# A Fourier mix and a gated feed-forward on one core: first columns in halves, one weight copy moved, last products in another order

## The chip, the cores and the metric

The kernel runs on one core of a Trainium2 chip. The metric is the device time in microseconds (us). The profile's span, from the first to the last instruction, is about 1.85 us shorter (616.8 us of time had a span of 614.9). Engines: PE is TensorE, PEld its weight loads, DVE is VectorE, ACT is ScalarE, POOL is GpSimd, and SP is SyncE, which issues most of the transfers. "Clock" is the granted clock of TensorE, 1.00 for full and 0.50 for half.

## The reference

```python
X = np.fft.fft(x, axis=1)            # x: 8 x 3008 x 256
X = np.fft.fft(X, axis=2)
h = X.real.reshape(24064, 256)
g, val = h @ w_gate, h @ w_val       # 256 x 1536 each
out = (gelu(g) * val) @ w_out        # 1536 x 256, float32
```

## The kernel before

The transform is done with matmuls: a fold of the input on VectorE (GpSimd for later batches), a first stage (`s1`), a second (`ch`, which gives the tile Z), and a turn (`tp_e`) that gives even columns E and odd columns O of 128 x tokens. The feed-forward needs, for each of 12 slices of the hidden width, a gate product (E, O, and O with "minus" weights for the mirrored tokens) and a value product. GELU runs on ScalarE, the products with it on VectorE and GpSimd, and layer 2 goes to `out`. The opening builds the first columns and a part of the weights; later work is put into numbered slots between the matmuls of the feed-forward.

The parts that matter here (cuts marked):

```python
def psum(tag):
    bufs = {"g": 2, "v": 3, "o": 1, "dft": 2}[tag]          # 8 banks
...
def osb_tile():
    return work([128, 2, C], FP32, "osb", 3, "out_sb")      # three output buffers
...
# opening(): warm matmuls keep TensorE busy before there is work
warm(16)
...
columns = t_columns()                                       # ten small matmuls
...
s1(0, 2, 0)(); s1(0, 2, 1)()
...
warm(6)
...
warm(1)
s1(0, 0, 0)(); s1(0, 0, 1, "V")()
make_w(0, 0, 256, m_at=minus, tag="o", copy_at=copies)()    # gate weights, matmuls only
t_write()
for pp in range(2):
    ch(0, pp, qs=(0,))(); ch(0, pp, "V", qs=(1,))()
copies.pop()()                                              # gate copy, ScalarE
make_w(1, 0, 256, m_at=minus, m_engine="V", tag="v", copy_at=copies)()
tp_e(0, 0, 0, "A", tag="v")()                               # E out by ScalarE
tp_e(0, 0, 1, "V", tag="dft")()                             # O out by VectorE
copies.pop()(); minus[0](); minus[1]()
...
# layer 2 of the very last chunk: sub = 128 tokens, sign 0 direct, sign 1 mirrored
subs = [nsub - 1, *range(nsub - 1)] if last(ci) else range(nsub)
...
if last(ci):
    osb = osb_tile()
    if sign == 0:   # VectorE copies, both stores issued by SyncE
    else:           # ScalarE copies, first store by ScalarE, second by SyncE
```

## Time and profile before

The time is 616.64 us (median of 3 runs, 616.6 to 617.27). I cut the span at events: each is the start of an instruction, except the Z copy, which counts from its end. (The yw matmuls are twelve one-column matmuls that stand in slot 6.)

| stretch, us | before |
|---|---|
| start to the first fold on VectorE (its loads have landed) | 8.26 |
| first fold to the end of the last Z copy by VectorE | 8.09 |
| last Z copy to the first value matmul | 1.82 |
| first value matmul to the yw matmuls (slot 6) | 12.72 |
| yw matmuls to the last layer-1 matmul | 568.56 |
| last layer-1 matmul to the last matmul | 11.19 |
| last matmul to the end | 4.29 |
| span | 614.93 |

In the lines of a timeline the columns are start, duration, engine, line, operation, output<-input, and in brackets the idle time before and what ended it. Here are two more lines of the kernel before that the argument needs later: the start of the first fold, and (last line) ScalarE's last output copy.

```profile
8.26 0.19 DVE L221 TENSOR_TENSOR eo_sb<-x_stage,xb 94x8 bf16<-94x8 f32 x1
...
610.95 0.38 ACT L794 ACTIVATE out_sb<-ps_g 128x256 f32<-128x256 f32 x1 [2.24 <-DMA out_dram<-out_sb]
```

### The profile page before, as it was taken

What the parts mean: (1) busy time and instruction counts of PE and PEld (TensorE: products, weight loads), DVE (VectorE), ACT (ScalarE), POOL (GpSimd) and SP (SyncE); (2) the same over time, 40 slices, a digit from 0 to 9 for tenths busy, and PEclk for the clock granted to TensorE, in tenths of its full rate; (3) what the DMA queues carried; (4) which work ended last, traced back from release to release, by engine and by line L of the source; (5) the groups of instructions that cost most, each with busy time, mean ns of one, the idle gap of its engine ahead of it and who ended that gap; (6) DMA issues with size and microseconds to landing.
All of it is one profiled execution on the core that took longest, in us unless ns stands there. A gap on an engine that the chain in (4) does not pass through costs nothing.

```text
span 614.9 us, 12747 instructions
## 1 busy us (share of the span) xinstructions
PE 605.4 (98%) x4181; PEld 406.9 (66%) x4229; DVE 577.3 (94%) x941; ACT 425.0 (69%) x824; POOL 508.9 (83%) x513
## 2 busy tenths in 40 slices
PE   8999999999999999999999999999999999999997
PEld 4466666666666666666666666666666666666666
DVE  8799999999999999999999999999999999999992
ACT  6888677777776777667766677666776676666661
POOL 8999899999987999789997899869997655565551
PEclk8999999999999999999999999999999999999999
DMA  9962834547253364532553344533213223111123
GB/s 175 200 137 57 237 95 117 141 116 189 80 144 92 100 163 119 140 100 58 157 150 94 106 107 107 146 102 100 64 49 77 62 87 78 42 46 47 37 51 83
DMA packets 52466, 65.40 MB, mean 106 GB/s; under 512 B 7629, under 2 KB 47278, under 8 KB 50004
## 3 DMA queue, kind: packets, MB, share of 16 engines
q1 hardware_dynamic: 45472, 49.03, 30.5%
q0 software_dynamic: 6608, 15.29, 11.7%
q8 instruction: 33, 0.54, 0.4%
q10 hardware_dynamic: 320, 0.26, 0.2%
q14 instruction: 33, 0.27, 0.2%
HBM read 39.65 MB, written 30.17 MB: 114 GB/s over the span
## 4 chain that ended last, share of the span: by engine, by line
PE 94%; DVE 2%; issue 1%; DMA 1%; ACT 1%; SPq 1%; POOL 0%; DVEq 0%; POOLq 0%; ACTq 0%
PE ps_o L778 39%; PE ps_g L681 29%; PE ps_v L681 20%; PE ps_dft L562 2%; PE ps_dft L598 2%; DMA out_dram<-out_sb 1%; PE ps_dft L451 1%; SPq L675 1%; PE ps_o L847 0%; PE ps_dft L542 0%; ACT gelu_sb L705 0%; ACT gelu_sb L714 0%; DVE v_sb L751 0%; POOL h_sb L753 0%; PE ps_dft L603 0%
## 5 line engine op out<-in xcount | busy, mean ns | idle before, releaser
L753 POOL TENSOR_TENSOR h_sb<-gelu_sb,v_sb 128x512 bf16<-128x512 bf16 (+1 forms) x280 | 319.9, 1147 | 87.0 <-DVE v_sb L751 79.0
L778 PE MATMUL ps_o<-Wo_sb,h_sb 128*128 128x256 bf16 (+1 forms) x2232 | 334.3, 272 | 0.0
L778 PEld LDWEIGHTS <-h_sb 128*128 128x128 bf16 (+1 forms) x2304 | 228.6, 100 | 111.2 <-POOL h_sb L753 1.0
L733 DVE SCALAR_TENSOR_TENSOR ve_sb<-EB_sb,yw,ps_v 128x512 f32<-128x512 bf16 (+1 forms) x280 | 206.3, 737 | 18.6 <-PE ps_v L681 16.6
L705 ACT ACTIVATE gelu_sb<-ps_g 128x512 bf16<-128x512 f32 (+1 forms) x288 | 169.3, 588 | 78.1 <-PE ps_g L681 62.9
L749 DVE TENSOR_TENSOR h_sb<-gelu_sb,ps_v 128x512 bf16<-128x512 bf16 (+1 forms) x280 | 190.0, 678 | 0.7
L681 PEld LDWEIGHTS <-W_sb 128*128 128x128 bf16 x1440 | 138.4, 98 | 78.0 <-issue 1.7
L751 DVE SCALAR_TENSOR_TENSOR v_sb<-ve_sb,ps_v 128x512 f32<-128x512 f32 (+1 forms) x280 | 187.4, 669 | 0.0
L714 ACT ACTIVATE gelu_sb<-ps_g 128x512 bf16<-128x512 f32 (+1 forms) x288 | 168.6, 585 | 0.0
L681 PE MATMUL ps_g<-O_sb,W_sb 128*128 128x512 bf16 (+1 forms) x530 | 159.1, 374 | 2.7 <-DVE O_sb L610 0.3
L681 PE MATMUL ps_g<-E_sb,W_sb 128*128 128x512 bf16 (+1 forms) x287 | 107.6, 375 | 0.7 <-ACT gelu_sb L714 0.5
L681 PE MATMUL ps_v<-O_sb,W_sb 128*128 128x512 bf16 (+1 forms) x288 | 108.0, 375 | 0.0
L681 PE MATMUL ps_v<-E_sb,W_sb 128*128 128x512 bf16 (+1 forms) x288 | 107.9, 375 | 0.0
L798 ACT ACTIVATE out_sb<-ps_o 128x512 f32<-128x512 f32 x92 | 55.0, 598 | 34.2 <-PE ps_o L778 34.1
L229 POOL TENSOR_TENSOR eo_sb<-ab_sb 94x512 bf16<-94x512 f32 (+1 forms) x70 | 77.7, 1112 | 0.4
L565 ACT ACTIVATE S_sb<-ps_dft 96x512 bf16<-96x512 f32 x56 | 33.2, 592 | 29.7 <-PE ps_dft L562 29.7
L222 POOL TENSOR_TENSOR ab_sb<-x_raw,x_raw 94x508 f32<-94x508 f32 (+1 forms) x30 | 33.0, 1101 | 0.0
L225 POOL TENSOR_TENSOR ab_sb<-x_raw,x_raw 94x508 f32<-94x508 f32 (+1 forms) x30 | 33.0, 1100 | 0.0
L562 PE MATMUL ps_dft<-eo_sb,G 94*96 94x256 bf16 x119 | 22.3, 272 | 0.0
L608 ACT ACTIVATE E_sb<-ps_dft 128x512 bf16<-128x512 f32 (+1 forms) x23 | 13.6, 590 | 12.0 <-PE ps_dft L598 12.0
L608 ACT ACTIVATE O_sb<-ps_dft 128x512 bf16<-128x512 f32 (+1 forms) x22 | 13.0, 590 | 11.6 <-PE ps_dft L598 11.1
L163 POOL DMA_INDIRECT x_raw<-in_x_dram,idx x18 | 17.2, 957 | 2.9 <-issue 0.8
(151 smaller groups left out, 207.6 us busy)
## 6 DMA issues: line engine op xcount, KB each, us to landing
out_dram<-out_sb SPq DMA_DIRECT2D x364, 64.0 KB
x_raw<-in_x_dram SPq DMA_DIRECT2D x10, 768.0 KB
Z_sb<-z SPq DMA_DIRECT2D x7, 768.0 KB
z<-S_sb SPq DMA_DIRECT2D x7, 576.0 KB
EB_sb<-yrow SPq DMA_DIRECT2D x6, 376.2 KB
z<-S_sb SPq DMA_DIRECT2D x7, 192.0 KB
x_raw<-in_x_dram SPq DMA_DIRECT2D x2, 640.0 KB
x_stage<-in_x_dram SPq DMA_DIRECT2D x1, 768.0 KB
```

Source lines behind the costliest of these rows:

```text
L229: eng.tensor_tensor(_sub(eo, [[C, nj], [1, 128]], j0 * C + g * 128), ab(0, 0, [[1, 128]]), ab(1, 0, [[1, 128]]), op=op)
L562: nc.tensor.matmul(ps[:96, q * C : (q + 1) * C], G[:, j, :], _sub(eo, [[1, C]], j * C), start=(j == js[0]), stop=(j == js[-1]))
L565: nc.scalar.activation(_sub(st["S"], [[1, 512]], (4 * jg + 2 * half) * C, part_num=96), ps[:96, :], AF.Copy)
L681: nc.tensor.matmul(ps[:, :n], W[nm, part][:, fs], src, start=start, stop=stop, **kw)
L705: nc.scalar.activation(gl[:, 0, :n], pg[:, :n], AF.Gelu)
L714: nc.scalar.activation(_sub(gl, [[-1, n]], TOK + n - 1), pg[:, :n], AF.Gelu)
L733: nc.vector.scalar_tensor_tensor(ve[:, :n], EB_bufs[b][:, c0 : c0 + n], yw[:, fc : fc + 1], pv[:, :n], op0=ALU.mult, op1=ALU.add)
L749: nc.vector.tensor_tensor(st["h"][:, fc, 0, :n], gl[:, 0, :n], pv[:, :n], op=ALU.mult)
L751: nc.vector.scalar_tensor_tensor(_sub(vv, [[-1, n]], n - 1), ve[:, :n], 2.0, pv[:, :n], op0=ALU.mult, op1=ALU.subtract)
L753: nc.gpsimd.tensor_tensor(st["h"][:, fc, 1, :n], gl[:, 1, :n], vv[:, :n], op=ALU.mult)
L778: nc.tensor.matmul(pso[:m, half], st["h"][:, fc, sign, h0 : h0 + m], Wo_sb[:, fc, :], start=(fc == 0 and not (first and sign)), stop=(fc = ...
L798: nc.scalar.activation(_sub(osb, [[1, 2 * C]], 0, part_num=m), pso[:m, :], AF.Copy)
```

## The change

Its intent: bring the first gate and value matmuls forward by taking E and O out of two banks each with both engines; use ScalarE's idle time for the gate copy; drop a warm matmul; relieve ScalarE of one minus copy; and in the last layer 2 put a group between the first one and the one that waits for GpSimd.

```diff
-    def tp_e(b, gi, g=0, engine="A", tag=None):
+    def tp_e(b, gi, g=0, engine="A", tag=None, part=slice(0, 4)):
 ...
-            for pair, o, n in pairs(gi):
+            for pair, o, n in pairs(gi)[part]:
                 nc.tensor.matmul(...)
             if b == 0 and g == 1:
-                for pair, o, n in pairs(gi):
+                for pair, o, n in pairs(gi)[part]:
                     nc.tensor.matmul(ps[0:1, o : o + n], ...)
-            n = chunk_len[gi]
-            dst = _sub(EO_bufs[b][g], [[1, n]], chunk_off[gi])
+            o, n = pairs(gi)[part][0][1], sum(w for _, _, w in pairs(gi)[part])
+            dst = _sub(EO_bufs[b][g], [[1, n]], chunk_off[gi] + o)
 ... (the copies read ps[:, o : o + n] for ps[:, :n])
-            subs = [nsub - 1, *range(nsub - 1)] if last(ci) else range(nsub)
-            l2s = [... for s in subs for g in range(2) for f in range(0, NFC, L2P)]
+            order = [(s, g) for s in range(nsub) for g in range(2)]
+            if last(ci):
+                order = [(nsub - 1, 0), (0, 0), (nsub - 1, 1), *order[1:-2]]
+            l2s = [... for s, g in order for f in range(0, NFC, L2P)]
 ...
-        warm(1)
         s1(0, 0, 0)()
 ...
         make_w(0, 0, 256, m_at=minus, tag="o", copy_at=copies)()
+        copies[0]()
         t_write()
 ...
-        copies.pop()()
         make_w(1, 0, 256, m_at=minus, m_engine="V", tag="v", copy_at=copies)()
-        tp_e(0, 0, 0, "A", tag="v")()
-        tp_e(0, 0, 1, "V", tag="dft")()
-        copies.pop()()
+        for g in range(2):
+            tp_e(0, 0, g, "A", tag="v", part=slice(0, 2))()
+            tp_e(0, 0, g, "V", tag="dft", part=slice(2, 4))()
+        copies[1]()
 ...
-                (2, make_w(0, 512, 512, (0,), "V")), (2, make_w(0, 512, 512, (1,))),
+                (2, make_w(0, 512, 512, (0,), "V")), (2, make_w(0, 512, 512, (1,), m_engine="V")),
```

More of the change, by code (lines that the diff above doesn't have):

```diff
@@ L601, in run @@
             if b == 0 and g == 1:
-                for pair, o, n in pairs(gi):
+                for pair, o, n in pairs(gi)[part]:
                     nc.tensor.matmul(
                         ps[0:1, o : o + n], st["Z"][:, pair, 128:129], _sub(TP, [[1, n]], 0), start=True, stop=True)
-            n = chunk_len[gi]
-            dst = _sub(EO_bufs[b][g], [[1, n]], chunk_off[gi])
+            o, n = pairs(gi)[part][0][1], sum(w for _, _, w in pairs(gi)[part])
+            dst = _sub(EO_bufs[b][g], [[1, n]], chunk_off[gi] + o)
             if engine == "A":
-                nc.scalar.activation(dst, ps[:, :n], AF.Copy)
+                nc.scalar.activation(dst, ps[:, o : o + n], AF.Copy)
             else:
-                nc.vector.tensor_copy(dst, ps[:, :n])
+                nc.vector.tensor_copy(dst, ps[:, o : o + n])
         return run
@@ L807, in ffn_work @@
                 ("G", l1_gate), ("V", l1_value), ("g", l1_gate2), ("v", l1_value2))}
-            subs = [nsub - 1, *range(nsub - 1)] if last(ci) else range(nsub)
-            l2s = [l2_piece(ci, s, g, f) for s in subs for g in range(2) for f in range(0, NFC, L2P)]
+            order = [(s, g) for s in range(nsub) for g in range(2)]
+            if last(ci):
+                order = [(nsub - 1, 0), (0, 0), (nsub - 1, 1), *order[1:-2]]
+            l2s = [l2_piece(ci, s, g, f) for s, g in order for f in range(0, NFC, L2P)]
             chunks.append((parts, l2s))
```

## The prediction

> **What bounds the kernel now.** I read the page first, then who waited for whom on TensorE (PE), then the busy time of stretches, then the timeline of the stretches that the diff touches.
>
> ```profile
> PE 605.4 (98%) x4181; PEld 406.9 (66%) x4229; DVE 577.3 (94%) x941; ACT 425.0 (69%) x824; POOL 508.9 (83%) x513
> ```
>
> PE is busy for 98% of the 614.9 us span. So a change gains only where PE is not streaming, or where it removes a matmul. Busy time hides short holes, so I ask for PE's waits and for the stretches:
>
> ```profile
> PE ps_g L681 <- ACT gelu_sb L714: 0.5, 1, 0.5
> PE ps_dft L778 <- POOL h_sb L753: 0.3, 1, 0.3
> PE ps_g L681 <- DVE O_sb L610: 0.3, 1, 0.3
> ```
> ```profile
> 10.30:13.70 3.40, 3.40 (x24) 2.06 (x23) 3.13 (x14) 3.37 (x8) 3.40 (x5) 0.50 1.21 166
> 60.00:600.00 540.00, 537.71 (x3724) 364.44 (x3765) 522.00 (x804) 376.48 (x726) 451.71 (x437) 1.00 0.39 103
> ```
>
> The columns of the waits are total, times, longest; of the stretches the length, then busy time of PE, PEld, DVE, ACT, POOL, then clock, DMA share, GB/s. The reader is to see that from 60 to 600 us PE is full at clock 1.00 (the 2.3 us missing are in part lost matmul records: a hole of exactly one 0.22 us matmul recurs). Nothing in the diff touches it. The whole stake lies in three holes: at 17 us (wait for the odd columns O), at 25 us (wait for a GELU) and at 602 us (wait for GpSimd's last product). Together they are under 2 us of 616.64, so the result can hardly leave the 2% band. The question is the sign and the tenths.
>
> **What the Trainium skill says.** "PSUM — Partial Sum Buffer", section "PSUM bank collisions raise a hardware error", says that two engines must not touch one bank (on the same quadrant of partitions) at once, two reads included, and that the scheduler makes such accesses wait for each other. The trace agrees:
>
> ```profile
> 31.91 0.60 ACT L459 ACTIVATE W_sb<-ps_dft 128x512 bf16<-128x512 f32 x1 [0.36 <-PE ps_dft L451]
> ...
> 32.55 0.75 DVE L477 TENSOR_SCALAR W_sb<-ps_dft,keep 128x512 bf16<-128x512 f32 x1 [0.41 <-ACT W_sb L459]
> ```
>
> VectorE's minus copy (L477), which only reads what ScalarE's copy (L459) reads, starts 0.04 us after that ends. This is why the change gives each half a bank of its own, and it is also what will hurt below. "TensorE: Matmul & The Clock Gate", sections "Part 1: The HAM clock gate" and "Back-to-back issue gap", says the clock is half or full, decided on windows of about 3.4 us, and the warm spacing is N/2.4 GHz + 2.5 ns. The trace agrees: 0.50 for the 3.4 us above, then 1.00, and the spacings after it are 0.056, 0.109 and 0.216 us for 128, 256 and 512 columns.
>
> **Part 1, warm matmul and gate copy.** The warm matmul starts at 13.41 us and the next (s1, third quarter of the columns) at 13.79: it holds PE 0.38 us at half clock. Its inputs were ready by 13.41. Without it the last two s1 groups take about 0.08 us a matmul until 13.74 and end 0.2 us earlier. But VectorE copies the second of them (14.33 to 14.89), and is busy with the one before until 14.21; with the usual overlap of about 0.05 us it can start at 14.17. Gain so far 0.16 us, and Z, made from it, comes 0.16 earlier: its last piece at 16.20 for 16.36. The gate copy (0.59 us) moves from 15.99 into ScalarE's empty time from 14.65 to 15.27. With part 1 it can run from 14.54 to 15.13, and the first Z copy is then wanted at 15.11: it just fits, and delays nothing.
>
> **Part 2, halves.**
>
> ```profile
> 16.67 0.60 ACT L608 ACTIVATE E_sb<-ps_v 128x512 bf16<-128x512 f32 x1
> ...
> 17.17 0.59 ACT L459 ACTIVATE W_sb<-ps_v 128x512 bf16<-128x512 f32 x1
> 17.21 0.69 DVE L610 CAST O_sb<-ps_dft 128x512 bf16<-128x512 f32 x1 [0.86 <-PE ps_dft L603]
> ...
> 17.65 0.48 ACT L475 ACTIVATE W_sb<-ps_o,keep 128x256 bf16<-128x256 f32 x1
> 17.82 0.48 DVE L477 TENSOR_SCALAR w_minus<-ps_v,keep 128x256 bf16<-128x256 f32 x1
> ```
>
> Today E goes out by ScalarE (to 17.27) and O by VectorE (to 17.90); the gate matmuls start at 17.32 and 17.96, the first value matmul at 18.17. From there PE streams without a hole until 24.9, so 18.17 is the date that matters. After the change, halves of 256 columns cost 0.38 on ScalarE and 0.43 on VectorE (the rows of Z copies, L548 and L550). PE: E halves issued by 16.25; O's two halves each have two one-column matmuls, and going between 128 and 1 columns costs a 0.147 us step instead of 0.056 (16.64 to 16.79 today), now three times: last O result at 16.79 for the first half, 17.19 for the second. ScalarE: E 16.32, O 16.83 to 17.21, value copy 17.11 to 17.70. VectorE: E to 16.94, O 17.23 to 17.66. The gate can start at 17.1 and its O part at 17.71: 0.25 earlier.
>
> But there are only three banks under the tag v. Counting them through the opening, today the two users after make_w's value bank are E and the first value product; that product gets a bank long free. Now both E and O take one, and the first value product gets the bank of make_w itself. It must wait for the value copy (17.70 on ScalarE), then, by the rule above, for VectorE's minus copy (17.76 to 18.24). So the value matmul starts at about 18.29, not 18.17: PE loses 0.12 us, and the halves' gain goes into this new wait. I give -0.12, plus or minus 0.2.
>
> **Part 3, one line of the weight plan.** The few words do not name it: the minus copy of make_w(0, 512, 512) goes from ScalarE to VectorE.
>
> ```profile
> 23.38 0.60 ACT L459 ACTIVATE W_sb<-ps_dft 128x512 bf16<-128x512 f32 x1 [0.62 <-PE ps_dft L451]
> 23.88 0.68 ACT L475 ACTIVATE W_sb<-ps_dft,keep 128x512 bf16<-128x512 f32 x1
> 24.45 0.60 ACT L705 ACTIVATE gelu_sb<-ps_g 128x512 bf16<-128x512 f32 x1
> 24.92 0.61 ACT L714 ACTIVATE gelu_sb<-ps_g 128x512 bf16<-128x512 f32 x1
> ```
> ```profile
> 25.58 0.38 PE L681 MATMUL ps_g<-E_sb,W_sb 128*128 128x512 bf16 x1 [0.51 <-ACT gelu_sb L714]
> ```
>
> ScalarE runs back to back, and PE waits for the bank that the second GELU reads. Without L475 the GELUs start at 23.88 and 24.36, the bank is free at 24.96, PE goes on at 25.01 (it is through with its own work at 24.91): 0.57 earlier. The next value matmul needs weights whose copy (L459, 25.40 today) cannot start before 25.10, its matmuls ending at 25.07; it starts at 25.76 for 26.23. So 0.47 stays. VectorE pays 0.75 us, in its idle 0.82 us before 25.08. Gain 0.47.
>
> **Part 4, last layer 2.**
>
> ```profile
> 601.08 1.36 PE L778 MATMUL ps_dft<-Wo_sb,h_sb 128*97 128x256 bf16 x11
> 602.74 0.31 PE L778 MATMUL ps_dft<-Wo_sb,h_sb 128*97 128x256 bf16 x1 [0.30 <-POOL h_sb L753]
> 602.89 0.27 PE L778 MATMUL ps_o<-Wo_sb,h_sb 128*128 128x256 bf16 x1
> ```
>
> Eleven matmuls at 0.109 end at 602.28; the twelfth needs GpSimd's product (602.69). Put a group of twelve (1.31 us) that needs only VectorE's product in between and nothing waits: 84 matmuls from 601.08 end at 610.25, where today the last group ends at 610.75 (from 609.44). PE gains 0.50. The output buffers could take it back, as there are three: the eighth and last product reuses that of the fifth, whose store landed at 610.44 today, 0.5 before the last copy (610.95). The fifth reuses that of the second, and waited for its store until 607.4 today; the new second product is an even one that needs no GpSimd, its copy out is at 602.6, its stores issue on SyncE at 603.95 and 604.5 behind earlier ones and land about 606.3 (1.7 after issue, as today). So the fifth goes out near 606.5 and its store lands near 609.5, before the last product is done. So the gain reaches the last store: 0.50. The skill's "DMA: Bandwidth & Descriptors", section "Anatomy of one DMA", puts about 2 us of fixed cost on a transfer, mostly the receipt; here the last was issued at 611.36 and landed at 613.60, and that tail is unchanged.
>
> **Sum.** +0.12 - 0.47 - 0.50 = -0.85: 616.64 to 615.8 us.
>
> **Rivals.** (a) The bank wait is not as I count it, and the gate's 0.25 us comes through: 615.4. For: DVE O_sb is the wait on record. Against: the count of banks and the 32.55 line. (b) The warm matmul held the clock up: if the window that decides after it is judged idle, a further 3.4 us go at half clock, and up to 1.5 us of PE work is added: 617. Against: the other six warm matmuls and s1 fill that window (3.40 of 3.40 busy, of which the one removed is a tenth). (c) PE's early stretch is held by GpSimd or a DMA behind it, and what comes before 25 us is swallowed: 616.1, only the tail staying. Against: PE has no wait on either between 25 and 600 us. (d) VectorE's extra 0.75 us pushes its products and PE's value banks: loses up to 0.3: 616.1.
>
> **Range and chances.** The three runs of before spread over 0.67 us, as much as the gain; the free phase of the clock windows may be why. The rivals span 615.4 to 617, so 8 in 10: 615.2 to 616.6. 2% would be 12.3 us: 99% within.
>
> **What would show it.** PE's wait at 25.6 for L714 gone or under 0.1; the wait at 602.7 gone; the first value matmul waiting for L477 on ps_v near 18.3; the clock still 1.00 from 13.7. Wrong if the clock stays at half past 14 us, if the value matmul starts before 18.0, or if a new PE wait appears after 26 us.

## The result, and the profile after

The changed kernel took 616.75 us (median of 4 runs, 615.78 to 617.67); the kernel before 616.72 us (4 runs, 616.6 to 617.27). The ratio is 0.9999 with a 95% interval from 0.998 to 1.0017: the same. A ratio is the mean time of one kernel's runs over that of the other's runs of the same rounds, so it is not quite the ratio of the medians. The prediction was 615.8 us, with a range up to 616.6: it missed, by little, and the reasons are worth more than the miss.

The page after, and TensorE's waits over the whole span:

```profile
PE 606.2 (99%) x4228; PEld 405.7 (66%) x4228; DVE 577.7 (94%) x943; ACT 424.8 (69%) x824; POOL 508.5 (83%) x513
```
```profile
PE ps_g L520 <- DVE eo_sb L222: 2.0, 1, 2.0
...
PE ps_dft L520 <- DVE eo_sb L222: 0.7, 1, 0.7
PE ps_v L520 <- DVE eo_sb L225: 0.3, 1, 0.3
```

All three holes of before (for O, for the GELU, for GpSimd) are gone from the list. Those that stand here are for the first folds, in the first 13 us. By this view the change did what it was meant to do. For O the list deceives, though: it leaves out what is under 0.15 us, and the trace before has lost the record of the second even gate matmul (287 of 288 are there), which makes its hole look longer. From the first even gate matmul to the odd one it is 0.64 us before (17.32 to 17.96) and 0.59 after (18.02 to 18.61), so this hole shrank by 0.05 us only. (The 47 additional matmul records are not work: this trace lost fewer.) So why is the time the same? The stretches, in two traces of the changed kernel (the second is the experiment after_again):

| stretch, us | before | after | after_again |
|---|---|---|---|
| start to first fold | 8.26 | 9.31 | 8.25 |
| first fold to last Z copy | 8.09 | 7.76 | 8.00 |
| to first value matmul | 1.82 | 1.77 | 1.77 |
| to the yw matmuls | 12.72 | 12.23 | 12.23 |
| to the last layer-1 matmul | 568.56 | 568.57 | 568.57 |
| to the last matmul | 11.19 | 10.69 | 10.68 |
| to the end | 4.29 | 5.05 | 5.12 |
| span | 614.93 | 615.38 | 614.62 |

Two gains of half a microsecond are there, in the fourth and the sixth stretch. The last stretch gives back 0.76 and 0.83 us. And the first two stretches differ by up to 1.06 us between two traces of the same kernel.

**The start.** The first fold in the first trace after:

```profile
9.31 0.19 DVE L221 TENSOR_TENSOR eo_sb<-x_stage,xb 94x8 bf16<-94x8 f32 x1 [0.98 <-DMA xb<-in_x_dram,idx]
```

VectorE waited 0.98 us for the first gather from memory, which no part of the change touches; in after_again it did not. The clock was another matter of chance. This line answers to the one of before at 0.50:

```profile
10.30:13.70 3.40, 2.41 (x24) 1.16 (x22) 3.37 (x12) 2.53 (x4) 3.40 (x5) 1.00 1.23 175
```

**The halves.** The predicted wait for a bank did not come:

```profile
18.13 0.42 DVE L610 CAST O_sb<-ps_dft 128x256 bf16<-128x256 f32 x1 [0.31 <-issue]
18.61 0.48 DVE L477 TENSOR_SCALAR w_minus<-ps_v,keep 128x256 bf16<-128x256 f32 x1
```
```profile
18.02 0.61 PE L681 MATMUL ps_g<-E_sb,W_sb 128*128 128x512 bf16 x2
18.61 0.39 PE L681 MATMUL ps_g<-O_sb,W_sb 128*128 128x512 bf16 x1
18.84 0.38 PE L681 MATMUL ps_v<-E_sb,W_sb 128*128 128x512 bf16 x1
```

The value matmul at 18.84 starts right after the odd gate matmul, while VectorE's minus copy (18.61 to 19.09) still reads make_w's bank. So they cannot share a bank. No trace names the banks, but the program as built does: the allocator gives the bank that was released longest ago, and that is the bank of E's first half.

**The weight plan.** ScalarE's row and TensorE's next gate matmul:

```profile
24.05 0.60 ACT L459 ACTIVATE W_sb<-ps_dft 128x512 bf16<-128x512 f32 x1 [0.62 <-PE ps_dft L451]
24.54 0.59 ACT L705 ACTIVATE gelu_sb<-ps_g 128x512 bf16<-128x512 f32 x1
25.02 0.61 ACT L714 ACTIVATE gelu_sb<-ps_g 128x512 bf16<-128x512 f32 x1
```
```profile
25.68 0.38 PE L681 MATMUL ps_g<-E_sb,W_sb 128*128 128x512 bf16 x1
```

L475 is gone from between the copy and the GELUs, and the gate matmul starts 0.05 us after the second GELU ends, 0.10 us late instead of 0.67.

**The end.** TensorE in the new order, and ScalarE's output copies:

```profile
601.26 1.47 PE L778 MATMUL ps_o<-Wo_sb,h_sb 128*128 128x256 bf16 x12
602.57 1.47 PE L778 MATMUL ps_dft<-Wo_sb,h_sb 128*97 128x256 bf16 x12
```
```profile
604.45 0.38 ACT L794 ACTIVATE out_sb<-ps_dft 97x256 f32<-97x256 f32 x1 [3.75 <-DMA out_dram<-out_sb]
...
609.80 0.38 ACT L794 ACTIVATE out_sb<-ps_dft 128x256 f32<-128x256 f32 x1 [3.74 <-DMA out_dram<-out_sb]
...
611.09 0.38 ACT L794 ACTIVATE out_sb<-ps_g 128x256 f32<-128x256 f32 x1 [0.91 <-DMA out_dram<-out_sb]
```

And VectorE's copies of the fifth and the seventh product:

```profile
607.97 0.42 DVE L791 COPY out_sb<-ps_v 128x256 f32<-128x256 f32 x1 [4.77 <-DMA out_dram<-out_sb]
...
610.17 0.42 DVE L791 COPY out_sb<-ps_o 128x256 f32<-128x256 f32 x1 [1.78 <-DMA out_dram<-out_sb]
```

TensorE runs through. But three of ScalarE's four copies now wait for a store, and two of VectorE's. The third product is complete at 604.04 (602.57 + 1.47), and its copy starts at 604.45, because the third output buffer in turn is that of the last product of the chunk before, whose store landed at 604.34. The sixth is complete at 607.97 (its group starts at 606.50) and waits until 609.80: its buffer is that of the third product, whose second store has 31 rows, was issued by SyncE at 606.46 and landed at 609.70. Ahead of it on SyncE one store issue took 1.70 us, where the others take about 0.5. The fifth is complete at 606.66 and copied at 607.97: its buffer is that of the second product, whose second store, the one with the long issue, landed at 607.85. The eighth is complete at 610.59 and copied at 611.09, after the fifth's last store landed at 610.98. The seventh is complete at 609.28 and copied at 610.17, and its late stores then stand before the last one on SyncE: the last copy ends at 611.47, but the last store is issued at 612.05 (before, 0.02 us after the end of the copy). It lands at 614.04; before, the last store was issued at 611.36 and landed at 613.60.

### The profile page after: what moved, and what is told of

Read it like the earlier page. It is cut to its first block, busy times and chain, and to the rows that moved or that the text cites. A ratio compares the mean times of both kernels' runs of the same rounds, so it can differ in the third digit from the quotient of the medians.

```text
span 615.4 us, 12787 instructions
## 1 busy us (share of the span) xinstructions
PE 606.2 (99%) x4228; PEld 405.7 (66%) x4228; DVE 577.7 (94%) x943; ACT 424.8 (69%) x824; POOL 508.5 (83%) x513
## 4 chain that ended last, share of the span: by engine, by line
PE 95%; DMA 2%; ACT 1%; DVE 1%; SPq 0%; issue 0%; POOL 0%; ACTq 0%; DVEq 0%; POOLq 0%
PE ps_o L778 40%; PE ps_g L681 30%; PE ps_v L681 20%; PE ps_dft L562 2%; PE ps_dft L598 2%; DMA xb<-in_x_dram,idx 1%; DMA out_dram<-out_sb 1%; PE ps_dft L451 1%; PE ps_dft L542 0%; SPq L675 0%; PE ps_v L778 0%; ACT L426 0%; DVE eo_sb L222 0%; DVE out_sb L791 0%; PE ps_dft L603 0%
## 5 line engine op out<-in xcount | busy, mean ns | idle before, releaser
L681 PE MATMUL ps_g<-O_sb,W_sb 128*128 128x512 bf16 (+1 forms) x576 | 169.0, 375 | 0.0
```

What stands on the lines that cost most here:

```text
L681: nc.tensor.matmul(ps[:, :n], W[nm, part][:, fs], src, start=start, stop=stop, **kw)
```

## The experiments

All kernels gave the right result, and all runs count as fast by the 1.5% rule. "Before" is always the kernel before in the same rounds on the same chip. Medians are given, but the scatter of single runs (616.29 to 619.20 us for 28 runs of the kernel before) is larger than every effect here, so the verdicts rest on the stretches, of one trace each. On time alone, only best2 has an interval that leaves out 1. The diffs are cut to the lines that matter.

| stretch, us | reorder_only | plan_only | halves_only | warm_copy_only | after_old_tail | after_out4 | warm_more | warm_fit | best | best2 |
|---|---|---|---|---|---|---|---|---|---|---|
| first fold | 8.26 | 8.25 | 8.25 | 8.25 | 8.25 | 8.25 | 8.25 | 8.81 | 8.25 | 8.25 |
| to last Z | 9.70 | 7.61 | 7.61 | 9.21 | 7.68 | 7.80 | 8.11 | 7.95 | 7.61 | 8.28 |
| to value | 2.24 | 1.82 | 1.77 | 2.12 | 1.77 | 1.77 | 1.82 | 1.82 | 1.76 | 1.77 |
| to yw | 12.76 | 12.23 | 12.72 | 12.72 | 12.23 | 12.23 | 12.72 | 12.72 | 12.23 | 12.23 |
| to last layer 1 | 569.72 | 568.44 | 568.55 | 568.55 | 568.55 | 568.85 | 568.56 | 568.56 | 568.86 | 568.57 |
| to last matmul | 10.69 | 11.19 | 11.18 | 11.19 | 11.19 | 10.68 | 11.19 | 11.19 | 10.69 | 10.69 |
| to end | 4.65 | 4.28 | 4.29 | 4.29 | 4.29 | 4.29 | 4.31 | 4.31 | 4.30 | 4.33 |
| span | 618.02 | 613.82 | 614.38 | 616.34 | 613.96 | 613.87 | 614.95 | 615.37 | 613.70 | 614.12 |

### The parts alone

**reorder_only**: the kernel before with the new order of the last layer 2 and nothing else.

```diff
+                order = [(nsub - 1, 0), (0, 0), (nsub - 1, 1), *order[1:-2]]
```

> Only the last layer 2 in the new order, the rest as before. My theory from the two traces: TensorE gains 0.50 us between its last layer-1 matmul and its last matmul (11.19 us before, 10.69 after), but the stretch from its last matmul to the end of the span grows from 4.29 us to about 5.05, because the third product now needs the output buffer of the chunk before, and the slow 31-row store comes later on SyncE. So this part alone makes the time 0.2 to 0.3 us longer. Rival: the longer end was chance (one store issue took 1.70 us in that one trace); then the stretch stays near 4.3 us and the time falls by 0.5 us.

Measured: 616.33 us (615.92 to 619.85), before 617.25, ratio 0.9982 (0.9959 to 1.0005). TensorE gains 0.50 us and the end grows by 0.36, less than the 0.76 expected, so this part alone gained 0.14 us in this trace where I expected a loss. The long store issue is there again (1.28 us). The mechanism holds; its size varies from trace to trace. The same trace shows what scatter means:

```profile
10.76:17.59 6.83, 6.40 (x44) 4.24 (x43) 4.79 (x17) 4.56 (x11) 6.22 (x10) 0.50 1.24 182
```

For 6.83 us, two clock windows, TensorE had half clock, and the last Z copy came 9.70 us after the first fold. This trace has one more wait that the others lack, 0.9 us near 80 us for Z read back from memory (most of what makes the 569.72).

**plan_only**: one minus copy from ScalarE to VectorE.

```diff
+                (2, make_w(0, 512, 512, (0,), "V")), (2, make_w(0, 512, 512, (1,), m_engine="V")),
```

> Only the minus copy of one gate piece moved from ScalarE to VectorE. Theory: the wait of 0.67 us before the fifth even gate matmul shrinks to 0.1 us, the stretch from the first value matmul to the yw matmuls goes from 12.72 to 12.23 us, and nothing else moves: the span falls by 0.5 us against a trace with the same start. Rival: the 0.49 us seen after came from the changed start (halves, copy first), then the stretch stays at 12.7 us.

Measured: 616.92 us (615.66 to 618.57), before 617.25, ratio 1.0 (0.9971 to 1.0029). The stretch is 12.23 us: the whole 0.49 us comes from this line, and nothing behind it takes it back.

**halves_only**: E and O in halves, the copies where they were.

```diff
-        tp_e(0, 0, 0, "A", tag="v")()
-        tp_e(0, 0, 1, "V", tag="dft")()
+        for g in range(2):
+            tp_e(0, 0, g, "A", tag="v", part=slice(0, 2))()
+            tp_e(0, 0, g, "V", tag="dft", part=slice(2, 4))()
```

> Only the first even and odd columns in halves. Theory: the first value matmul gets a free bank (the allocator gives the bank released longest ago, not the next in turn), so there is no loss, but the halves gain almost nothing: from the end of the last Z copy to the first even gate matmul 0.95 us (0.97 before), to the first odd one 1.54 (1.61 before), to the first value matmul 1.77 (1.82 before). The rival of the prediction, a wait for the minus copy, would show 1.9 to 2.0 us to the first value matmul. A third view, that halves are worth their 0.25 us and something else ate them after, would show 1.55 us.

Measured: 616.55 us (616.22 to 618.87), before 617.25, ratio 0.9998 (0.9968 to 1.0027). From the last Z copy it is 0.96 us to the even gate matmul (0.97 before), 1.54 to the odd one (1.61) and 1.77 to the value matmul (1.82). The halves are worth 0.05 us. Half a copy is not half the time (0.42 us for 256 columns against 0.69 for 512 on VectorE), and the one-column matmuls are now visited twice, with a step of 0.147 us at each change.

**warm_copy_only**: no `warm(1)`, the gate copy ahead of the `ch` stage.

```diff
-        warm(1)
         s1(0, 0, 0)()
 ...
+        copies.pop()()
         t_write()
 ...
-        copies.pop()()
```

> Only the warm matmul taken out and the gate copy moved ahead. Theory: where the clock is at half around 13 us as in the trace before, the last Z copy ends about 0.15 us earlier after the first fold (7.95 for 8.09 us); where the clock is full there, 7.75 as after. The value stretch after it stays 1.8 us. The time of the first fold (8.26 us before, 9.31 after) is set by the landing of the first loads, which no part of the change touches, and it will scatter by several tenths between these four traces. Rival: taking out the warm matmul, or the copy, moves the first fold itself; then 9.3 us here and 8.3 us in the other three.

Measured: 616.73 us (616.34 to 618.17), before 617.25, ratio 0.9986 (0.9963 to 1.0008). The profiled run fell on two half-clock windows (10.85 to 17.67 us), so its 9.21 us says nothing on the part. Its first fold is at 8.25 us as in the other three, so the late one in the first trace after was chance. The part is read better from after_old_tail, which contains it and had full clock: 7.68 us to the last Z copy against 7.61 in plan_only and halves_only, which keep the warm matmul and had full clock too. At full clock it gains nothing. There the warm matmul takes 0.22 us, and VectorE, busy with its own folds, holds up the path.

### The tail and the clock

**after_again**: the changed kernel once more.

> The changed kernel once more, for a second trace. Theory: the first fold is at 8.25 us (9.31 in the first trace was a late landing by chance); from the first value matmul to the yw matmuls 12.23 us and from the last layer-1 matmul to the last matmul 10.69 us, both as in the first trace to 0.03; the stretch after the last matmul is again longer than the 4.29 us of before, somewhere from 4.6 to 5.1 us. Rival: it is near 4.3 us, and the first trace was chance there too.

Measured: 616.57 us (615.48 to 618.37), before 616.8, ratio 1.0001 (0.998 to 1.0023). All as the theory said, 5.12 us at the end included. Not every run can have this: the fastest had a span of 613.6 us, and the shortest stretches seen in any trace (8.25 + 7.61 + 1.76 + 12.23 + 568.44 + 10.68 = 608.97) leave at most 4.6 us for its end, where 5.1 stood in the two traces. So the loss varies from 0.3 us or less to 0.8 us.

**after_old_tail**: the changed kernel with the old order.

```diff
-                order = [(nsub - 1, 0), (0, 0), (nsub - 1, 1), *order[1:-2]]
+            subs = [nsub - 1, *range(nsub - 1)] if last(ci) else range(nsub)
```

> The changed kernel with the order of the last layer 2 of before. Theory: 11.19 us from the last layer-1 matmul to the last matmul, and 4.29 us after it, as before; the rest as after. Against the changed kernel with equal clock in the opening the span is then between 0.26 us shorter and 0.14 longer. Rival (the end is set by matmuls): 0.5 us longer.

Measured: 616.41 us (615.8 to 617.59), before 616.8, ratio 1.0001 (0.9984 to 1.0017). 11.19 and 4.29 us at the end: together 0.26 and 0.32 us shorter than in the two traces of the changed kernel, although TensorE waits for GpSimd here.

**after_out4**: the changed kernel with a fourth output buffer (an early weight tile, `w_minus`, uses the same set of buffers, so its line changes too).

```diff
-        return work([128, 2, C], FP32, "osb", 3, "out_sb")
+        return work([128, 2, C], FP32, "osb", 4, "out_sb")
```

> The changed kernel with four output buffers for three. Theory: the third product no longer waits for the last store of the chunk before, nor the sixth for the slow 31-row store; 10.69 us to the last matmul and 4.3 to 4.4 us after it, so 0.3 to 0.7 us shorter at the end than the changed kernel. Rival: SyncE's row of store issues, each about 0.5 to 0.6 us, is what holds the end; then 4.6 us or more stays after the last matmul.

Measured: 616.13 us (615.51 to 616.61), before 616.8, ratio 0.9991 (0.9975 to 1.0008). The last copies:

```profile
607.27 0.38 ACT L794 ACTIVATE out_sb<-ps_dft 128x256 f32<-128x256 f32 x1 [2.24 <-PE ps_dft L778]
...
609.89 0.38 ACT L794 ACTIVATE out_sb<-ps_g 128x256 f32<-128x256 f32 x1 [2.24 <-PE ps_g L778]
```

They wait for TensorE, not for a store, and the end is 4.29 us again with the 0.50 us kept. The long issue on SyncE is still there (1.32 us), so it alone does not hold the end; the shortage of buffers did. One side effect: between the yw and the last layer-1 matmuls TensorE has four holes of 0.15 us before an even gate matmul, where every three-buffer trace has two (near 270 and 567 us in most; elsewhere in plan_only and halves_only). The two more, near 97 and 213 us, are the 0.3 us.

**warm_more**: the kernel before with more warm matmuls.

```diff
         columns = t_columns()
+        warm(8)
 ...
-        warm(6)
+        warm(8)
```

> The kernel before with eight more warm matmuls after the small column matmuls, and eight for six after the first two s1 groups. Theory: the scatter of every kernel from 616 to 619 us comes from how many windows of 3.4 us in the opening TensorE gets at half clock (mean clock 1.000 for none, 0.997 for one, 0.994 for two); with TensorE kept busy there no window drops, the mean clock is 0.998 or more in all runs, the runs lie within 0.6 us of each other, and their median is 616.2 to 616.5 us, 0.4 to 1 us under the kernel before of the same rounds. Rival: the scatter comes from the landing of the first loads or from elsewhere; then it stays 1.5 us or more. A second rival: the added matmuls delay the s1 groups and cost as much as they gain; then the last Z copy ends later than 7.7 us after the first fold at full clock.

Measured: 616.79 us (616.28 to 617.41), before 616.8, ratio 1.0001 (0.9985 to 1.0018). The part of the theory that concerns the clock holds: mean clock 0.999 or 1.000 in all four runs, where the seven runs of before had 0.994 to 1.000. The rest failed: the runs lie 1.13 us apart, not within 0.6, so the windows are not the whole scatter, and the median is that of before. The second rival holds: eight matmuls delay the first s1 group to 10.36 us and ScalarE after it, and the last Z copy ends 8.11 us after the fold, at full clock.

**warm_fit**: four instead of eight after the small matmuls.

> The kernel before with four (not eight) more warm matmuls after the small column matmuls, and eight for six after the first two s1 groups. Theory: four at full clock (0.86 us) fit before the first s1 group needs TensorE, so nothing is delayed, and no window drops: mean clock 0.998 or more in every run, the last Z copy ends 7.6 to 7.7 us after the first fold (8.11 with eight), the runs lie within 0.7 us of each other, and the median is 0.3 to 0.8 us under the kernel before of the same rounds. Rival: the half-clock windows cost less than their company suggests (the fold chain on VectorE is the path anyway), and the median stays within 0.2 us of before. If four are too few to hold the clock, runs with 0.997 or less remain.

Measured: 616.52 us (616.28 to 617.2), before 616.86, ratio 0.9997 (0.9982 to 1.0011). Mean clock 0.998 or more in all five runs, which lie within 0.92 us of each other, more than the 0.7 I expected. Its profiled run had late loads again: the first fold at 8.81 us, and a second wait of VectorE for a gather later (0.8 us in both). So the landing of the loads is a second source of scatter, one that a warm clock does not cure. On time alone the run does not separate its theory from its rival.

### Versions that beat both

**best**: the changed kernel, four output buffers, the warm matmuls of warm_fit.

> The changed kernel with four output buffers and the warm matmuls of the other run of this call. Theory: the parts add up: 12.23 us from the first value matmul to the yw matmuls, 10.69 us from the last layer-1 matmul to the last, 4.29 after it, and no half-clock window; span near 613.3 us and time near 615.2 us in all runs, 1.3 to 1.8 us under the kernel before (ratio 0.9972 to 0.998). Rival: the opening's gain and the others do not add, because an earlier start runs into a load or into GpSimd; then the stretch from the yw matmuls to the last layer-1 matmul grows beyond 568.7 us and the time stays above 615.8.

Measured: 615.81 us (615.52 to 617.15), before 616.86, ratio 0.9989 (0.9976 to 1.0003). The parts at the end and in the weight plan add up in the trace (613.70 us), but the expected 615.2 us in all runs was missed, and both signs of the rival came, if barely: 568.86 us in the middle (over 568.7) and a median of 615.81 (over 615.8). The 568.86 us is the fourth buffer's 0.3 us again. Three of six runs were slower than 615.6 us, at mean clocks of 0.998 to 1.000, and no trace shows why.

**best2**: the changed kernel with the warm matmuls of warm_fit and three output buffers; the last chunk's odd products go to tiles that are idle by then.

```diff
-                    osb = osb_tile()
+                    osb = work([128, 2, C], FP32, "ve", 3, "out_ve") if sign else osb_tile()
```

> The changed kernel with the warm matmuls of the run before, three output buffers, and the four odd products of the last chunk put into the three ve buffers, which nobody needs by then. Theory: both four-buffer traces spent 568.85 us between the yw matmuls and the last layer-1 matmul against 568.56 in the others, in two holes of 0.15 us near 97 and 213 us, so the fourth buffer costs 0.3 us in the middle; with the ve buffers that stretch is 568.57 us, the stretches at the end are 10.69 and 4.3 us, and the time of runs with a first fold at 8.25 us is 615.2 us (615.5 with the fourth buffer). Rival: the holes belong to the store order at the end or to chance; then 568.85 us stays. A second rival: the ve buffers make the last products wait; then more than 4.5 us after the last matmul.

Measured: 615.41 us (615.32 to 615.96), before 616.94, ratio 0.9978 (0.9964 to 0.9991). The middle is 568.57 us again and the end 4.33. This is the best version: its slowest run is faster than all nine runs of before in the same rounds (616.29 to 619.16). Its profiled run was its slowest (615.96 us): VectorE waited 0.5 us for a load at 11.4 us. How much of its gain comes from the warm matmuls and how much from the other parts was not separated.

## Why the prediction was wrong

**What bounds the kernel, and the three holes**: right, but for the hole for O, which a lost record made look longer (above). TensorE fills the middle, and its stretch is 568.5 to 568.6 us in nearly all three-buffer traces. The suspicion of lost records was right as well: the trace after has TensorE busy for all 540.00 us between 60 and 600 us.

**Part 1, warm matmul and gate copy, 0.16 us**: mis-sized. It was worked out from a trace at half clock, where that matmul takes 0.38 us. At full clock there is no gain to see (7.68 against 7.61 us). In the only pair of traces with one half window around 10 to 14 us it is 0.09 (8.00 against 8.09).

**Part 2, "-0.12"**: the step that failed is "the first value product gets the bank of make_w itself". I took the three banks to be handed out in turn. In the built program they are handed out by who was released first, and in the trace no wait arose (18.84 us, above). Measured 0.05 us gained for the halves. Without the wait my own figures would have given 0.09 (0.25 less the 0.16 of part 1).

**Part 3, 0.47 us**: right, mechanism and size (0.49). It is the largest gain of the change that stays, and the few words on the change do not name it.

**Part 4, 0.50 us**: right for TensorE (0.50 and 0.51 us), wrong for the time. The failed step is "So the gain reaches the last store". I followed the buffers of the fifth and the eighth product only, and expected their stores too early: "1.7 after issue, as today" is misread, as the 64-row stores of before landed 1.9 us or more after their issue began. The second product's second store landed at 607.85 for the 606.3 that I gave it, so the fifth product was copied at 607.97 for 606.5, its last store landed at 610.98 for 609.5, and the eighth waited for it. Besides, the third meets the last store of the chunk before, and the sixth the slow 31-row store, which the new order moves one product later and puts behind two others on SyncE. The end grew by 0.36 to 0.83 us in the three traces, and after_out4 shows that it is the buffers: with a fourth the end is 4.29 us again.

**The sum.** With first folds at 8.25 us and full clock the stretches give, for the kernel before, 8.25 + 7.61 + 1.82 + 12.72 + 568.56 + 11.19 + 4.29 = 614.44 us of span, and for the changed one 8.25 + 7.68 + 1.77 + 12.23 + 568.57 + 10.69 + 5.08 = 614.27, with the mean of its two ends. This estimate from the measured stretches is a gain of 0.2 us, and of 0.6 where the end grows by 0.36 only (4.65 for 5.08), not of 0.85.

**The range**: failed on its own account. I took three runs of before, 0.67 us apart, for the scatter; 28 runs spread over 2.9 us. I suspected the clock windows and did not follow them: three runs of before at mean clock 0.994, which marks two half-clock windows, took 617.98 to 619.20 us, and seven at 0.999 or more 616.29 to 617.39. Rival (b) named the right part of the chip. The drop itself cannot come from the removed warm matmul (13.4 us): the windows after which the clock dropped lie between 5.6 and 10.9 us. Whether that matmul helps to bring the clock back is less clear. In warm_copy_only, without it, the window of 10.85 to 14.26 us did not bring the clock back, but that of 10.77 to 14.18 us in reorder_only, which has it, did not either. A mean clock of 0.995 or less, which marks two half-clock windows, came in 3 of 20 runs of the five kernels without it and in 6 of 37 with it (warm_more, warm_fit, best and best2 left out), so no loss is seen.

Left open: why the first loads sometimes land up to a microsecond late, what makes one store issue on SyncE take 1.3 to 1.7 us, why a fourth output buffer comes with two more holes in the middle, and which of the buffer waits at the end costs most.

## What to carry to other kernels

When an order of work changes near the end, list for every product which earlier store must land before its buffer is free, the previous chunk's included; a TensorE that runs through proves nothing if the last store is what ends the span. Cut two traces at the same few events before comparing them: gains of 0.5 us were plain in the stretches when the times of single runs differed by 3 us. A thinly filled stretch at the start can cost more than its length when it lets the clock drop: runs of before with two half-clock windows took 2.3 us longer. Warm matmuls kept the clock up here, but they have to fit before the real work is ready (eight were too many), and a gain in time from them alone was not shown.

## What the Trainium skill lacked or had wrong

- "TensorE: Matmul & The Clock Gate", section "Part 1: The HAM clock gate (the "warmup" mystery)": it says that a busy window raises the clock and an idle one drops it, not how busy. I counted each matmul's columns at 0.216 us for 512 (the spacing at full clock; twice that at half) in the 3.41 us windows of the clock record. The clock dropped after windows with 1.2 to 1.5 us of such streaming (before, after_again, reorder_only, warm_copy_only, after_out4) and stayed after windows with about 1.5 us (after, halves_only, after_old_tail). It did not come back after windows with 2.6 us (reorder_only, warm_copy_only) and came back after 3.1 to 3.3 us (before, after_again, after_out4). So a window that is far from idle can drop it, and more is needed to regain it; where the limits lie these traces do not tell. The page also says that the ramp is under 1% of a typical span; that agrees (the three runs of before with two dropped windows averaged 618.8 us against a median of 616.46 for the seven with none, 0.4%), but these 2.3 us are more than the whole gain of the best version (1.5).
- "DMA: Bandwidth & Descriptors", section "Anatomy of one DMA — SWDGE (gpsimd) path": it gives about 2.0 us of fixed cost plus bytes over bandwidth, for transfers that GpSimd issues. The output stores here are issued by SyncE and ScalarE. The last store of 64 rows, by SyncE, landed 2.2 us after its issue, close to that; but the smaller store of 31 rows (31 KB) landed 3.1 us (before) and 3.2 us (after) after its issue, so bytes alone do not set the time.
- "PSUM — Partial Sum Buffer", section "PSUM bank collisions raise a hardware error": nothing lacking; the copies that share a bank waited for each other (in the trace after, the minus copy at 18.61 us came after the value copy that ended at 18.57).
- No page gives a time for the step of 0.147 us between matmuls with 128 and with 1 weight column (0.056 us without the change of width), measured at 16.64 to 16.79 us before.
